# Moving P@V, both units' scores and the sine to even slots in a fused top-k attention and cosine-gated feed-forward kernel

## The chip, the cores and the metric

The kernel runs on one core of a Trainium2 chip. The metric is the device time of one execution in microseconds (us); the time of the kernel before is the median of three runs. Beside the times there is a profile of one execution, with the start and duration of each instruction on each engine: PE is the matrix engine (PEld its loading of weights), DVE the vector engine, ACT the scalar engine, POOL the general-purpose engine, SP the engine that issues most of the transfers.

## The reference

Top-k attention on 8 batches, 8 heads, 576 tokens, head dimension 64, followed by a feed-forward block on the 4608 x 512 result:

```python
scores = scale * np.matmul(q, k.transpose(0, 1, 3, 2))
kth = np.partition(scores, -top_k, axis=-1)[..., -top_k:-top_k + 1]   # top_k = 32
scores = np.where(scores >= kth, scores, -1000000000.0)
scores = scores - np.max(scores, axis=-1, keepdims=True)
attn = np.exp(scores)
attn = attn / (np.sum(attn, axis=-1, keepdims=True) + 1e-09)
x = np.matmul(attn, v)              # -> (4608, 512) after the heads are joined
h = x @ w_in                        # 512 x 2048
g = h * np.cos(h)
out = g @ w_out                     # 2048 x 512
```

## The kernel before

The work is cut into 144 **units**: 128 tokens by one pair of heads. Four units (`hp` 0 to 3) with the same tokens make a **block**, of which there are 36; one in nine lies across two batches, and its units have two `parts`. One unit starts per **slot**. In the long middle stretch a unit u has its top-k search on DVE in slot u, its mask and exponentials on ACT in slot u + 1, its normalisation and the way through DRAM that transposes it in the slots after, and then P@V for two units at once. When the four units of a block are through, its feed-forward is fed to PE in small items: eight "up" items (`ff1`) and eight "down" items (`ff2`) for each block. Each engine works through its instructions in the order in which the program issues them, so the order in `slot` is the order on each engine.

The way of a unit from the normalisation to P@V (`halves` has one buffer, `pT` three):

```python
    def normalise(u):
        s, rden = u["s"], u.pop("rden")
        for j in range(2):
            nc.gpsimd.tensor_scalar(
                out=s[:, j], in0=s[:, j], scalar1=rden[:, j : j + 1], scalar2=1.0,
                op0=ALU.mult, op1=ALU.mult,
            )

    def split(u):


        s = u.pop("s").rearrange("p j k -> p (j k)").bitcast(U16)
        halves = work.tile([P, 2, 2 * S], U16, tag="halves", name="halves", bufs=1)
        nc.gpsimd.tensor_copy(out=halves, in_=s.rearrange("p (k h) -> p h k", h=2))
        u["halves"] = halves

    def write_halves(u):
        rows = u["rows"] = dram.tile([P, 2, 2 * S], U16, tag="rows", name="rows")
        nc.sync.dma_start(out=rows, in_=u.pop("halves"))

    def transposes(u):
        rows = u.pop("rows").rearrange("q h k -> (q h) k")
        pT = u["pT"] = work.tile([P, 2 * NT + 1, P], F32, tag="pT", name="pT", bufs=3)
        words = pT.rearrange("p c q -> p (c q)").bitcast(U16)
        nc.sync.dma_start_transpose(
            out=words.rearrange("p (c q) -> p c q", c=2 * NT + 1), in_=rows
        )
    # ...
    def values(us):      # P@V of two units into one PSUM region: 20 matmuls for each unit
    # ...
```

The feed-forward between the two matmuls. `take_first` copies a bank from PSUM (`L478`); four up items fill one `g` tile; its sine argument is reduced on POOL, the sine taken on ACT, and the product taken on POOL:

```python
    def take_first(blk, g, mm, half):
        nc.scalar.mul(out=g[:, half * 512 : half * 512 + 512], in_=mm, mul=INV_2PI)
        if half == 1:
            fresh.append([blk, g])

    def take_banks():
        while full:
            take, *what = full.popleft()
            take(*what)

    def reduce_first():

        if not fresh:
            return
        blk, g = fresh[0]
        x = ffw.tile([P, 1024], F32, tag="x", name="x", bufs=XB)
        fresh[0].append(x)
        if ff["end"]:

            nc.vector.tensor_scalar(
                out=x, in0=g, scalar1=0.25, scalar2=MAGIC, op0=ALU.add, op1=ALU.add
            )
            nc.vector.scalar_tensor_tensor(
                out=x, in0=x, scalar=MAGIC, in1=g, op0=ALU.subtract, op1=ALU.subtract
            )
            return
        gp = nc.gpsimd
        gp.tensor_scalar(out=x, in0=g, scalar1=1.0, scalar2=0.25, op0=ALU.mult, op1=ALU.add)
        gp.tensor_scalar(out=x, in0=x, scalar1=1.0, scalar2=MAGIC, op0=ALU.mult, op1=ALU.add)
        gp.tensor_scalar(out=x, in0=x, scalar1=-MAGIC, scalar2=1.0, op0=ALU.add, op1=ALU.mult)

    def reduce_second():
        if not fresh or len(fresh[0]) < 3:
            return
        blk, g, x = fresh.popleft()
        if not ff["end"]:
            nc.gpsimd.tensor_tensor(out=x, in0=g, in1=x, op=ALU.subtract)
        waiting.append((blk, g, x, ff["now"], -TWO_PI_BELOW if ff["end"] else TWO_PI_BELOW))

    def sines(least):

        n = sum(c[3] < ff["now"] for c in waiting)
        if n == 0 or (n < least and waiting[0][3] + 2 > ff["now"]):
            return
        for _ in range(n):
            blk, g, x, _, scale = waiting.popleft()
            nc.scalar.activation(out=x, in_=x, func=AF.Sin, bias=halfpi, scale=scale)
            sined.append((blk, g, x))

    def gate(n):
        for _ in range(min(n, len(sined))):
            blk, g, x = sined.popleft()
            eng = nc.vector if ff["end"] else nc.gpsimd
            eng.tensor_tensor(out=g, in0=g, in1=x, op=ALU.mult)
            blk["gated"].append(ff["tick"])
```

How many items a slot feeds, and which (`tick` counts the calls of `feed`):

```python
    def can_first():
        if not first:
            return False
        blk, i = first[0]
        if blk["left"] or ff["tick"] < blk["tick"] + 2 or wq["ready"] < (((i + 1) * (256 // blk["w"]) - 1) // FC + 1) * NC:
            return False
        return i % 4 > 0 or ff["live"] + staged() < CHUNKS
    def can_second():
        if not second:
            return False
        blk, i, f = second[0]
        lag = 3 if 5 * NP < ff["now"] < NU - NP else 2
        gated = sum(ff["tick"] >= t + lag for t in blk["gated"])
        return gated * 1024 // blk["w"] >= f + 2 and wq["ready"] >= NC * NF // FC + f + 2
    def feed(n):
        ff["tick"] += 1
        while n > 0 and ff["credit"] >= 1:
            for kind in (ff["kind"], 1 - ff["kind"]):
                if (can_first, can_second)[kind]():
                    break
            else:
                return
            if kind == 0:
                ff1(*first.popleft())
            else:
                ff2(*second.popleft())
            if kind != ff["kind"] or ff["half"]:
                ff["kind"], ff["half"] = 1 - kind, 0
            else:
                ff["half"] = 1
            n, ff["credit"] = n - 1, ff["credit"] - 1
    # per slot: ff["credit"] = min(ff["credit"] + 5.0 - 0.9 * len(scored.get(i, [])), 5.3)
```

A slot of the middle stretch, and what it is called with:

```python
    EARLY, LAST = 2 * NP, NU - NP
    scored, last, last_values = {}, {}, {}
    for i, u in enumerate(units):
        two = i % 2 and EARLY + 2 < i < LAST + 2 and len(u["parts"]) == 1
        scored.setdefault(i - 2 if two else i - 1, []).append(u)
        for part in u["parts"]:
            last[part[0], u["hp"]] = i - 2 if two else i - 1
            last_values[part[0], u["hp"]] = i
    # ...
    def slot(i, u, w, x, y, z):
        if x:
            reciprocal(x)
        if u:
            topk_first(u, w)
            decode_second(2)
        if u:
            topk_round(u, 1)
            topk_round(u, 2)
            topk_round(u, 3)
        if z:
            values(z)
        made = scored.get(i, [])
        if z:
            take_banks()
        else:
            feed(1)
        for m in made:
            scores(m)
        late = len(made) > 0
        if w:
            bounds(w)
            mask(w)
        take_banks()
        if w and late:
            exponentials(w)
        if z:
            take_values(z)
        take_scores(units[i + 1])
        if w and not late:
            exponentials(w)
        for load, b, hp in at_slot.get(i, []):
            load(b, hp)
        load_weights(2)
        if y:
            transposes(y)
        gate(1)
        if x:
            normalise(x)
            split(x)
            write_halves(x)
        feed(2)
        take_banks()
        decode_third()
        decode_first(2)
        reduce_first()
        reduce_second()
        feed(1 if len(made) == 2 else 3)
        if i % 2:
            sines(1)
        elif i < EARLY + 8 or i > LAST - 2:
            sines(2)
    # ... the loop over the slots:
        u, w = (units[i - n] if 0 <= i - n < NU else None for n in range(2))
        x, y = (units[i - n] if EARLY <= i - n < LAST else None for n in range(2, 4))
        z = units[i - 5 : i - 3] if i % 2 and EARLY <= i - 5 < LAST else None
```

The first nine slots (`early_slot`) and the last four (`last_slot`) transpose on PE and use the same parts in another order.

Of the kernel before, what the change touches and what calls it, by code (L numbers as in the profile page):

```python
# [31 lines left out]
def kernel(  # L32
# [16 lines left out]
    NP = H // 2  # L49
# [35 lines left out]
    for i in range(DF // CW):  # L85
        w = consts.tile([P, NC, CW], F32, tag=f"w_in{i}", name=f"w_in{i}")
# [4 lines left out]
    for f in range(NF):  # L91
        w = consts.tile([P, DM], F32, tag=f"w_out{f}", name=f"w_out{f}")
# [3 lines left out]
    ff = {"live": 0, "tick": 0, "now": 0, "credit": 0.0, "end": False, "kind": 0, "half": 0, "open": 0}  # L96
# [58 lines left out]
    units = []  # L155
    for t0 in range(0, B * S, P):
        parts = []
# [183 lines left out]
    def reciprocal(u):  # L341
        u["rden"] = small.tile([P, 2], F32, tag="rden", name="rden")
        nc.vector.reciprocal(u["rden"], u.pop("den"))  # L343
# [19 lines left out]
# [11 lines that stand above are left out]
# [113 lines left out]
# [26 lines that stand above are left out]
            nc.gpsimd.tensor_tensor(out=x, in0=g, in1=x, op=ALU.subtract)  # L513
        waiting.append((blk, g, x, ff["now"], -TWO_PI_BELOW if ff["end"] else TWO_PI_BELOW))

    def sines(least):

        n = sum(c[3] < ff["now"] for c in waiting)
        if n == 0 or (n < least and waiting[0][3] + 2 > ff["now"]):
            return  # L520
        for _ in range(n):
# [10 lines that stand above are left out]
# [36 lines left out]
    def can_second():  # L568
        if not second:
            return False  # L570
        blk, i, f = second[0]

        lag = 3 if 5 * NP < ff["now"] < NU - NP else 2
        gated = sum(ff["tick"] >= t + lag for t in blk["gated"])
        return gated * 1024 // blk["w"] >= f + 2 and wq["ready"] >= NC * NF // FC + f + 2

# [18 lines that stand above are left out]
# [8 lines left out]
    EARLY, LAST = 2 * NP, NU - NP  # L603
    scored, last, last_values = {}, {}, {}
    for i, u in enumerate(units):
        two = i % 2 and EARLY + 2 < i < LAST + 2 and len(u["parts"]) == 1
        scored.setdefault(i - 2 if two else i - 1, []).append(u)
        for part in u["parts"]:
            last[part[0], u["hp"]] = i - 2 if two else i - 1
            last_values[part[0], u["hp"]] = i  # L610
    at_slot = {}
    order = [(b, hp) for b in range(B) for hp in range(NP)]
    for n in range(NP, len(order)):
        i = last[order[n - 5]] if n >= 5 else 0
        at_slot.setdefault(max(i, NP + 2), []).append((load_qk, *order[n]))
        i = last_values[order[n - 6]] if n >= 6 else 0
        at_slot.setdefault(max(i + 5 - i % 2, NP + 2), []).append((load_v, *order[n]))

    for hp in range(NP):
        at_slot.setdefault(hp, []).append((load_v, 0, hp))  # L620
# [44 lines left out]
        feed(2)  # L665
        sines(2)

    def slot(i, u, w, x, y, z):
        if x:
            reciprocal(x)  # L670
        if u:
# [29 lines that stand above are left out]
        for load, b, hp in at_slot.get(i, []):  # L701
            load(b, hp)
        load_weights(2)
        if y:
            transposes(y)
        gate(1)
        if x:
            normalise(x)
            split(x)
            write_halves(x)  # L710
        feed(2)
        take_banks()
        decode_third()
        decode_first(2)
        reduce_first()
        reduce_second()
        feed(1 if len(made) == 2 else 3)
        if i % 2:
            sines(1)
        elif i < EARLY + 8 or i > LAST - 2:  # L720
            sines(2)

    def last_slot(i, u, w, x, y, z):
        if x:
            reciprocal(x)
        if u:
# [9 lines that stand above are left out]
        if i + 1 < NU:  # L736
            scores(units[i + 1])
        if z:
            take_values(z)
        if i + 1 < NU:  # L740
            take_scores(units[i + 1])
        if y:
            transposes(y)
        if x:
            normalise(x)
            split(x)
            write_halves(x)
        reciprocal(w)
        normalise(w)
        if u:  # L750
            topk_round(u, 2)
            topk_round(u, 3)
        gate(2)
        feed(2)
        transposes_now(w)
# [4 lines that stand above are left out]
        values([w])  # L760
        take_values([w])
        feed(2)
# [10 lines left out]
    for i in range(NU + 1):  # L773
        ff["end"] = i >= NU
        ff["credit"] = min(ff["credit"] + 5.0 - 0.9 * len(scored.get(i, [])), 5.3)
        ff["now"] += 1
        wq["ready"] = wq["done"]
        u, w = (units[i - n] if 0 <= i - n < NU else None for n in range(2))
        x, y = (units[i - n] if EARLY <= i - n < LAST else None for n in range(2, 4))
        z = units[i - 5 : i - 3] if i % 2 and EARLY <= i - 5 < LAST else None  # L780
        if i <= EARLY:
            early_slot(i, u, w)
        elif i <= LAST:
            slot(i, u, w, x, y, z)
        else:
            last_slot(i, u, w, x, y, z)
    while first or second or full:
        ff["now"] += 1
        ff["credit"] = 2.0
# [44 lines left out]
```

## Time and profile before

| | us |
|---|---|
| median of three runs | 1522.23 (1521.3 to 1523.08) |
| span of the profiled execution | 1521.9 |
| busy: PE / DVE / ACT / POOL | 1417.3 / 1416.0 / 1149.2 / 1102.9 |
| one top-8 search of DVE (`MAX8`, 288 wide), mean | 0.447 |
| one fold of DVE (`L244`), mean | 0.752 |
| mean granted PE clock, share of full speed | 0.966 |

How to read the lines shown below. A line of the timeline gives the start, the time from the first start to the last end of a group, the engine, the line of the kernel, the operation with output and input, and how many instructions the group has; brackets name the idle time ahead of it and what ended that. In the table by stretch each engine has its busy time and, in brackets, its instructions; the last three numbers are the granted PE clock, the share of time in which the transfer engines were busy, and GB/s. The list of transfers ends with the median time from issue to landing. The list of waits has the total, the count and the longest. A down item is four instructions of `L543`, an up item sixteen of `L465`, since each matrix product shows as two instructions.

### The profile page before, as it was taken

To read this page: it belongs to the slowest core of one execution; us is meant where nothing else is said; L and a number is where in the kernel's file an instruction comes from. 1 tells how busy PE (TensorE), PEld (TensorE's weight loads), DVE (VectorE), ACT (ScalarE), POOL (GpSimd) and SP (SyncE) were. 2 spreads that over 40 slices of the span, in tenths; PEclk is the share of its full clock that TensorE was granted. 3 is DMA by queue.
4 is the path that set the end of the run, shared out by engine and by line. 5 is a ranking of instruction groups with operands and counts; after the bars stand their busy time and mean duration, and the time that the engine had idled before them with its cause. 6 is when DMAs were issued, how large, how long until landed. Compare 5 with 4: busy or idle time off the path is not lost.

```text
span 1521.9 us, 30207 instructions
## 1 busy us (share of the span) xinstructions
PE 1417.3 (93%) x10360; PEld 1020.5 (67%) x10360; DVE 1416.0 (93%) x4690; ACT 1149.2 (76%) x2322; POOL 1102.9 (72%) x837
## 2 busy tenths in 40 slices
PE   4567798999999999999999999999999999999899
PEld 3365365676777767777777767777777767776774
DVE  7989999999999999999999999999999999999521
ACT  7888766777777778877777777777777777777631
POOL 4777966778777778777777777777777777776500
PEclk6587999999999999999999999999999999999899
DMA  8422364645655555646655456555664455545000
GB/s 265 139 83 83 99 178 135 186 117 175 161 169 132 132 148 164 179 132 156 165 170 132 132 151 168 171 133 152 167 171 132 132 151 158 151 132 132 17 15 14
DMA packets 371753, 212.20 MB, mean 139 GB/s; under 512 B 321296, under 2 KB 337936, under 8 KB 371600
## 3 DMA queue, kind: packets, MB, share of 16 engines
q1 hardware_dynamic: 366192, 200.63, 48.7%
q10 hardware_dynamic: 5408, 9.65, 1.9%
q8 instruction: 81, 1.33, 0.4%
q14 instruction: 72, 0.59, 0.1%
HBM read 45.09 MB, written 87.29 MB: 87 GB/s over the span
## 4 chain that ended last, share of the span: by engine, by line
DVE 74%; PE 12%; ACT 6%; issue 3%; POOL 2%; DMA 2%; SPq 1%; DVEq 0%; ACTq 0%; POOLq 0%
DVE top L304 33%; DVE rest L307 27%; DVE rest L244 11%; PE o L543 5%; PE mm L465 4%; PE rim L408 2%; ACT s L334 1%; DVE top L292 1%; ACT s L326 1%; DVE top L297 1%; DVE w_out L138 1%; PE sc L220 1%; DMA pT<-rows 1%; DVE rden L343 1%; ACT st L127 1%
## 5 line engine op out<-in xcount | busy, mean ns | idle before, releaser
L304 DVE MAX8 top<-rest 128x8 f32<-128x288 f32 (+1 forms) x1656 | 681.2, 460 | 0.0
L465 PEld LDWEIGHTS mm<-xT,w_in 128*128 128x128 f32 x4608 | 536.3, 193 | 83.4 <-ACT g L478 39.8
L465 PE MATMUL mm<-xT,w_in 128*128 128x128 f32 x4608 | 546.9, 277 | 7.4 <-ACT g L478 3.4
L543 PE MATMUL o<-w_out,g 128*128 128x512 f32 x1152 | 532.1, 605 | 11.3 <-POOL g L530 5.6
L307 DVE MATCH_REPLACE8 rest<-top,rest 128x288 f32<-128x288 f32 (+1 forms) x1104 | 494.6, 455 | 0.0
L348 POOL TENSOR_SCALAR s<-s,rden 128x576 f32<-128x576 f32 x288 | 212.7, 750 | 259.1 <-DVE rden L343 259.1
L543 PEld LDWEIGHTS o<-w_out,g 128*128 128x128 f32 x1152 | 209.3, 192 | 232.4 <-issue 210.4
L360 POOL COPY halves<-s 128x2304 uint16<-128x2304 uint16 x132 | 277.7, 2103 | 27.4 <-DMA rows<-halves 19.9
L334 ACT ACTIVATE s<-s,nd 128x576 f32<-128x576 f32 x288 | 219.7, 764 | 0.8
L244 DVE TENSOR_TENSOR rest<-sc,s 128x576 f32<-128x576 f32 x264 | 198.5, 752 | 10.2 <-ACT s L231 2.7
L326 ACT ACTIVATE s<-s,nb 128x576 f32<-128x576 f32 x288 | 205.3, 760 | 0.0
L314 ACT ACTIVATE nb<-top 128x4 f32<-128x4 f32 x144 | 29.6, 206 | 230.2 <-DVE top L297 229.6
L408 PE MATMUL rim<-pT,v 128*64 128x128 f32 (+1 forms) x2560 | 163.1, 272 | 21.5 <-ACT pT L389 13.7
L530 POOL TENSOR_TENSOR g<-g,x 128x1024 f32<-128x1024 f32 x67 | 158.3, 2363 | 22.3 <-ACT nb L314 11.4
L220 PE MATMUL sc<-k,q 64*128 64x448 f32 (+1 forms) x640 | 150.1, 583 | 17.0 <-DMA k<-in_k_dram 9.3
L513 POOL TENSOR_TENSOR x<-g,x 128x1024 f32<-128x1024 f32 x68 | 161.0, 2367 | 5.7
L408 PEld LDWEIGHTS rim<-pT,v 128*64 128x64 f32 x2560 | 134.4, 141 | 38.3 <-ACT pT L389 16.3
L230 ACT COPY s<-sc 128x896 f32<-128x896 f32 x144 | 129.0, 896 | 3.3 <-PE sc L220 3.3
L478 ACT ACTIVATE g<-mm 128x512 f32<-128x512 f32 x144 | 83.7, 583 | 54.3 <-PE mm L465 43.9
L220 PEld LDWEIGHTS rim<-k,q 64*128 64x128 f32 (+1 forms) x640 | 57.3, 180 | 57.8 <-issue 52.7
L523 ACT ACTIVATE x<-x,halfpi 128x1024 f32<-128x1024 f32 x72 | 82.5, 1149 | 6.9 <-DVE x L499 6.1
L523 ACT ACT_TABLE_LOAD x66 | 84.7, 1283 | 1.6 <-ACT ob L553 0.4
(55 smaller groups left out, 1232.0 us busy)
## 6 DMA issues: line engine op xcount, KB each, us to landing
rows<-halves SPq DMA_DIRECT2D x132, 576.0 KB, 3.2
out_dram<-ob ACTq DMA_DIRECT2D x36, 256.0 KB, 2.9
q<-in_q_dram SPq DMA_DIRECT2D x31, 288.0 KB, 3.3
st<-in_moe_w_in_dram SPq DMA_DIRECT2D x16, 512.0 KB, 5.8
v<-in_v_dram SPq DMA_DIRECT2D x32, 256.0 KB, 3.9
st<-in_moe_w_out_dram SPq DMA_DIRECT2D x16, 512.0 KB, 3.6
k<-in_k_dram SPq DMA_DIRECT2D x31, 144.0 KB, 3.4
k<-in_k_dram SPq DMA_DIRECT2D x32, 128.0 KB, 3.8
```

The source lines that it names most:

```text
L220: nc.tensor.matmul(to[r0 : r0 + rows, j, 0 : k1 - k0], st["q"][d, q0 : q0 + rows], st["k"][d, k0:k1], start=True, stop=True,)
L244: nc.vector.tensor_tensor(out=u["rest"][:, :, i * HS : (i + 1) * HS], in0=sc[:, :, 0:HS], in1=s[:, :, HS:S], op=op,)
L304: nc.vector.max(to[:, j], src[:, j])
L307: nc.vector.match_replace(rest[:, j], to[:, j], src[:, j], NEG)
L326: nc.scalar.activation(out=s[:, j], in_=s[:, j], func=AF.Prelu, bias=nb[:, j, 1:2], scale=SCALE, alpha=FAR)
L334: nc.scalar.activation(out=s[:, j], in_=s[:, j], func=AF.Exp, bias=nd[:, j : j + 1], scale=1.0, accum_out=den[:, j : j + 1],)
L348: nc.gpsimd.tensor_scalar(out=s[:, j], in0=s[:, j], scalar1=rden[:, j : j + 1], scalar2=1.0, op0=ALU.mult, op1=ALU.mult,)
L360: nc.gpsimd.tensor_copy(out=halves, in_=s.rearrange("p (k h) -> p h k", h=2))
L408: nc.tensor.matmul(o[d, to], lhsT, rhs, start=c == 0, stop=c == NT)
L465: nc.tensor.matmul(mm[:, at : at + w], w_in[f // FC][:, c, (f % FC) * P : (f % FC + 1) * P], blk["xT"][:, c], start=c == 0, stop=c == NC - 1,)
L523: nc.scalar.activation(out=x, in_=x, func=AF.Sin, bias=halfpi, scale=scale)
L543: nc.tensor.matmul(o, g[:, at : at + P], w_out[f], start=f == 0, stop=f == NF - 1)
```

## The change

P@V of a pair of units and the scores of two units move from odd to even slots, and P@V is taken one slot earlier after its units' normalisation. The transpose is issued in the same slot as the write that it reads. In even slots the argument of the sine is computed ahead of the normalisation, and the sine follows at the end of the same slot. The wait of down items for the product (`lag`) is lengthened from slot 12 on instead of slot 20. It is meant to shorten the way from a unit's scores to the feed-forward.

```diff
--- before.py
+++ after.py
@@ -513,9 +513,9 @@
             nc.gpsimd.tensor_tensor(out=x, in0=g, in1=x, op=ALU.subtract)
         waiting.append((blk, g, x, ff["now"], -TWO_PI_BELOW if ff["end"] else TWO_PI_BELOW))
 
-    def sines(least):
-
-        n = sum(c[3] < ff["now"] for c in waiting)
+    def sines(least, since=1):
+
+        n = sum(c[3] <= ff["now"] - since for c in waiting)
         if n == 0 or (n < least and waiting[0][3] + 2 > ff["now"]):
             return
         for _ in range(n):
@@ -570,7 +570,7 @@
             return False
         blk, i, f = second[0]
 
-        lag = 3 if 5 * NP < ff["now"] < NU - NP else 2
+        lag = 3 if 3 * NP < ff["now"] < NU - NP else 2
         gated = sum(ff["tick"] >= t + lag for t in blk["gated"])
         return gated * 1024 // blk["w"] >= f + 2 and wq["ready"] >= NC * NF // FC + f + 2
 
@@ -603,7 +603,7 @@
     EARLY, LAST = 2 * NP, NU - NP
     scored, last, last_values = {}, {}, {}
     for i, u in enumerate(units):
-        two = i % 2 and EARLY + 2 < i < LAST + 2 and len(u["parts"]) == 1
+        two = i % 2 == 0 and EARLY + 2 < i < LAST + 2 and (len(u["parts"]) == 1 or u["hp"] == 0)
         scored.setdefault(i - 2 if two else i - 1, []).append(u)
         for part in u["parts"]:
             last[part[0], u["hp"]] = i - 2 if two else i - 1
@@ -614,7 +614,7 @@
         i = last[order[n - 5]] if n >= 5 else 0
         at_slot.setdefault(max(i, NP + 2), []).append((load_qk, *order[n]))
         i = last_values[order[n - 6]] if n >= 6 else 0
-        at_slot.setdefault(max(i + 5 - i % 2, NP + 2), []).append((load_v, *order[n]))
+        at_slot.setdefault(max(i + 4 - i % 2, NP + 2), []).append((load_v, *order[n]))
 
     for hp in range(NP):
         at_slot.setdefault(hp, []).append((load_v, 0, hp))
@@ -665,7 +665,7 @@
         feed(2)
         sines(2)
 
-    def slot(i, u, w, x, y, z):
+    def slot(i, u, w, x, z):
         if x:
             reciprocal(x)
         if u:
@@ -701,26 +701,29 @@
         for load, b, hp in at_slot.get(i, []):
             load(b, hp)
         load_weights(2)
-        if y:
-            transposes(y)
-        gate(1)
+        if i % 2 == 0:
+            reduce_first()
+            reduce_second()
         if x:
             normalise(x)
             split(x)
             write_halves(x)
+            transposes(x)
+        gate(1)
         feed(2)
         take_banks()
         decode_third()
         decode_first(2)
-        reduce_first()
-        reduce_second()
+        if i < EARLY + 8:
+            reduce_first()
+            reduce_second()
         feed(1 if len(made) == 2 else 3)
-        if i % 2:
+        if i % 2 == 0:
+            sines(1, 0)
+        elif i < EARLY + 8:
             sines(1)
-        elif i < EARLY + 8 or i > LAST - 2:
-            sines(2)
-
-    def last_slot(i, u, w, x, y, z):
+
+    def last_slot(i, u, w, x, z):
         if x:
             reciprocal(x)
         if u:
@@ -739,12 +742,11 @@
             take_values(z)
         if i + 1 < NU:
             take_scores(units[i + 1])
-        if y:
-            transposes(y)
         if x:
             normalise(x)
             split(x)
             write_halves(x)
+            transposes(x)
         reciprocal(w)
         normalise(w)
         if u:
@@ -776,14 +778,14 @@
         ff["now"] += 1
         wq["ready"] = wq["done"]
         u, w = (units[i - n] if 0 <= i - n < NU else None for n in range(2))
-        x, y = (units[i - n] if EARLY <= i - n < LAST else None for n in range(2, 4))
-        z = units[i - 5 : i - 3] if i % 2 and EARLY <= i - 5 < LAST else None
+        x = units[i - 2] if EARLY <= i - 2 < LAST else None
+        z = units[i - 4 : i - 2] if i % 2 == 0 and EARLY <= i - 4 < LAST else None
         if i <= EARLY:
             early_slot(i, u, w)
         elif i <= LAST:
-            slot(i, u, w, x, y, z)
+            slot(i, u, w, x, z)
         else:
-            last_slot(i, u, w, x, y, z)
+            last_slot(i, u, w, x, z)
     while first or second or full:
         ff["now"] += 1
         ff["credit"] = 2.0
```

## The prediction

> **What bounds the kernel now.** I read the busy times first, then the busy time by stretch, then one pair of slots in the timeline, engine by engine.
>
> ```profile
> PE 1417.3 (93%) x10360; PEld 1020.5 (67%) x10360; DVE 1416.0 (93%) x4690; ACT 1149.2 (76%) x2322; POOL 1102.9 (72%) x837
> ```
>
> Two engines are level, so an average does not tell which one is the bound. By stretch:
>
> ```profile
> 200.00:400.00 200.00, 184.72 (x1480) 135.06 (x1477) 194.99 (x683) 146.55 (x309) 145.40 (x109) 0.98 0.58 160
> ...
> 600.00:800.00 200.00, 199.87 (x1541) 146.39 (x1540) 198.86 (x694) 159.99 (x323) 157.73 (x117) 1.00 0.60 160
> ...
> 1440.00:1480.00 40.00, 40.00 (x261) 29.86 (x260) 9.69 (x11) 14.66 (x29) 6.40 (x6) 1.00 0.02 7
> ```
>
> The columns are PE, PEld, DVE, ACT, POOL. In the middle both PE and DVE are full; in the last 80 us PE works alone on feed-forward left over. Is PE's fullness real? One pair of slots:
>
> ```profile
> 810.16 1.04 PE L408 MATMUL rim<-pT,v 128*64 128x128 f32 x16
> ...
> 813.50 3.70 PE L543 MATMUL o<-w_out,g 128*128 128x512 f32 x8
> 817.04 3.73 PE L465 MATMUL mm<-xT,w_in 128*128 128x128 f32 x32
> 820.61 3.60 PE L543 MATMUL o<-w_out,g 128*128 128x512 f32 x8
> 824.27 3.84 PE L465 MATMUL mm<-xT,w_in 128*128 128x128 f32 x32
> 828.04 1.10 PE L408 MATMUL rim<-pT,v 128*64 128x128 f32 x16
> ```
>
> The groups start back to back, and the same 32 and 8 instructions take as long in the tail, where nothing holds them. So it is real. The pair repeats after 828.04 - 809.02 = 19.02 us (809.02 is the start of the first unit's P@V); the vector engine's slots start at 800.77, 810.29 and 819.79, also 19.02 a pair. PE has eight feed items in a pair (813.50 to 828.04, so 1.82 us each), P@V of two units and scores of two: 18.98 us. **PE can be delayed once, but it can never catch up.** The last `L465` group of a pair ends just ahead of the next P@V; it completes a `g` tile. Next the Pool engine:
>
> ```profile
> 810.53 1.47 POOL L348 TENSOR_SCALAR s<-s,rden 128x576 f32<-128x576 f32 x2 [3.64 <-DVE rden L343]
> 812.06 2.10 POOL L360 COPY halves<-s 128x2304 uint16<-128x2304 uint16 x1
> 814.13 1.04 POOL L504 TENSOR_SCALAR x<-g 128x1024 f32<-128x1024 f32 x1
> ...
> 817.53 2.37 POOL L513 TENSOR_TENSOR x<-g,x 128x1024 f32<-128x1024 f32 x1
> 819.93 2.36 POOL L530 TENSOR_TENSOR g<-g,x 128x1024 f32<-128x1024 f32 x1
> 822.28 1.47 POOL L348 TENSOR_SCALAR s<-s,rden 128x576 f32<-128x576 f32 x2
> ```
>
> Normalise and split take 3.6 us from start to end. Sine's argument (four instructions) takes 819.93 - 814.13 = 5.80. Now it stands **behind** the normalisation, so nothing of attention waits for it. The way out of Pool is write, then transpose:
>
> ```profile
> 806.92 0.34 SPq L365 DMA_DIRECT2D rows<-halves  x1
> 809.77 3.20 SPq L371 DMA_TRANSPOSE pT<-rows  x1
> ```
>
> ```profile
> pT<-rows SPq DMA_TRANSPOSE x132, 4.8
> POOL halves L360 <- DMA rows<-halves: 19.9, 14, 4.6
> ```
>
> The transpose goes out 2.85 us after the write, as soon as that has landed, and lands 4.8 us later in the median (4.3 to 6.9). The second line: `halves` has one buffer, and a split close behind another already waits for the write.
>
> [...] a normalisation emitted behind a product `L530` starts behind it (822.28 above). So what is moved ahead of the normalisation holds it. [...]
>
> **The change, part by part.**
>
> *Transpose issued with its write.* Same instructions. Before, it stood a slot later in the program but already left at 2.85 us behind its write. Alone it is worth nothing; it only no longer has the next slot's loads in front of it.
>
> *P@V and both scores in even slots, P@V one slot earlier.* Same instructions. In slot i PE now takes units i-4 and i-3, where it took i-5 and i-4. The gain: a block's feed-forward starts a slot earlier. Stepping through `feed`'s credits and ticks by hand from slot 9 on, I get 476 items open at slot 35 before and 469 after (slot 17 is blocked in the new order, but later losses vanish). Both then do exactly eight a pair (three with P@V, five without, with the credit capped at 5.3), so the lead of seven stays to the end: 7 x 1.82 = **12.7 us less tail**. The `lag` of 3 from slot 12 on is met exactly by gates of the slot before last and stops nothing later. The cost: unit i-3 is normalised in slot i-1 and needed at once. In an undisturbed odd slot, normalise starts 0.24 us after the slot, the write goes at 3.9, the transpose at 6.75, landing at 11.4, and a slot is 9.5: ready 1.9 us **into** the next slot, while PE came to the second unit 0.13 us ahead of it (810.16 against 810.29). So PE falls back at least 2 us against DVE; that much the buffers between scores and the folds take up.
>
> *Sine's argument ahead of the normalisation.* In even slots Pool first takes `g`, whose last matmuls end just ahead of that slot's P@V, and only then normalises. This closes a **loop**: P@V of the odd unit -> the eight items -> `g` -> argument -> even unit's split -> odd unit's split -> write -> transpose -> P@V two pairs on. Its length:
> - second unit's P@V to the end of the eight items: 828.04 - 810.16 = 17.88
> - copy of `g` from PSUM 0.58 and two handovers of some 0.08: 0.73
> - argument 5.80; even normalise and split 3.63: 9.43
> - the odd split waits until the even write has landed (`halves`): 2.90; the split: 2.10
> - the queue is then still in the even transpose (2.90 + 2.6 against 5.00): 0.50
> - the odd write landed, behind a transpose (241.95 to 245.39 in the queue's timeline): 3.44
> - transpose landed: 4.6
>
> Sum 41.6 us for two pairs, where DVE needs 38.04. **The loop is 3.5 us too long**, so a pair takes 20.8 us, 1.75 more. If the two transfers don't hold each other up, it is 40.5, or 20.25 a pair: 1.2 more. I take the middle, 1.5. From slot 20 (full rate) to 140 there are 60 pairs: 90 us, less some 2 us that PE may fall back before DVE waits.
>
> *Sine beside the scores.* Sine follows its argument in the same even slot. It was beside the two scores before as well, with two table loads a pair (1.28 us each); this stays, only in the other slot. Pool's argument would be ready 6.5 us after `g`, about when ACT gets there. No cost of its own.
>
> **Sum.** 1522.2 + 90 - 2 - 12.7 = 1597.5; I say 1598.
>
> **The rivals.**
> 1. *The loop does not bind.* The change then brings its 12.7 us: about 1510. For it: each earlier stage shortens the pipeline, and the lag fits the new order exactly. Against it: it asks the loop to be 3.5 us shorter than durations measured in this very trace. One way would be that the feed ended a pair with `o` and not with `mm` items: `g` would be ready 3.6 us earlier. By hand I find the order 22 1 | 1 22 11 (1 for up, 2 for down), with `mm` last, as in the trace above.
> 2. *It binds a little*, say 0.5 us a pair, if the `halves` wait and the queue's wait vanish because DVE's own delay spreads the two splits: 30 - 12.7, about 1540.
> 3. *ACT becomes the bound*: `g` is copied first in an even slot, ahead of the thresholds, so a late PE also delays mask, exponentials and the copy of the next scores. From `g` to the end of that copy I count some 6.2 us, so DVE starts odd slots no earlier. This is how the loop reaches DVE and no second loss.
>
> **Range and chances.** The loop at 20.25 to 20.9 a pair gives 1580 to 1620; a looser one 1540 to 1580; none 1510. The first is by far the likeliest, so 1538 to 1624 for eight in ten. Faster by over 2% (below 1492) would take far more than the tail can give: 0.03. Within 2% (to 1552.7): rival 1 and the lower part of rival 2, 0.17. Slower: 0.80.
>
> **What would show it.** Right: a pair near 20.5 us in the middle; PE waiting at P@V for `pT<-rows`, about 1.5 us a pair; DVE waiting once a pair at the fold `L244` for the copy of the scores; Pool waiting for `L478` ahead of `L504`, and at the split for `rows<-halves`; the stretch after the last slot some 12 us shorter. Wrong: pairs of 19.02 with P@V waiting once and not again (rival 1); DVE waiting elsewhere, for `den` or `nb`, with `pT` long landed; or a tail that is not shorter, which would make my count of items wrong.

## The result, and the profile after

The kernel after the change takes 1708.8 us (median of four runs, 1702.94 to 1711.04) against 1522.47 us for the kernel before, measured beside it: a ratio of **1.122 (95% interval 1.119 to 1.1248)**, slower by 186 us. The prediction was 1598 us, with 1538 to 1624 as its range. The direction and the mechanism came as predicted; the size did not.

The busy times after:

```profile
PE 1475.0 (87%) x10360; PEld 1063.7 (63%) x10360; DVE 1420.9 (84%) x4689; ACT 1161.6 (68%) x2326; POOL 1106.3 (65%) x838
```

The vector engine (DVE) does the same work in nearly the same time (1416.0 before), and it is no longer full. The matrix engine (PE) has the same 10360 instructions but is busy 58 us longer, so some of them have become slower. Two lines make up 55 of the 58 us: P@V (`L408`, 163.1 us before and 187.7 after) and the scores (`L220`, 150.1 and 180.7). By stretch (columns as before: PE, PEld, DVE, ACT, POOL, then the granted PE clock):

```profile
200.00:400.00 200.00, 170.75 (x1275) 124.12 (x1276) 169.12 (x591) 132.03 (x268) 125.55 (x93) 0.91 0.49 132
600.00:800.00 200.00, 180.09 (x1334) 129.51 (x1330) 167.03 (x582) 134.59 (x269) 130.94 (x98) 0.93 0.49 133
```

In the middle no engine is full any more. A stretch in which every engine has gaps is bound by a chain that runs through several of them. The waits after, as engine, line, releaser, total us, count, longest:

```profile
POOL x L504 <- ACT nb L314: 280.7, 62, 8.5
...
POOL halves L360 <- DMA rows<-halves: 145.8, 64, 7.0
...
PE rim L408 <- DMA pT<-rows: 144.8, 51, 5.5
DVE rest L244 <- ACT s L231: 140.6, 37, 7.6
```

They stood at 4.5 (put down to `L478` itself), 19.9, 3.4 and 2.7 us before. The first three belong to one ring: Pool's argument waits for `g` (the scalar engine's `L314` follows `L478` by 0.1 us and is named for it), the split waits for the write, and P@V for the transpose. The fourth hangs on it: DVE waits for scores that PE made too late. One passage of that ring, from the chain of waits of the kernel after (start, us, what):

```profile
1122.40 2.40 PE rim L408 x20
...
1139.08 3.59 PE mm L465 x32
...
1142.68 0.60 ACT g L478
...
1143.38 1.05 POOL x L504
...
1146.78 2.37 POOL x L513
1149.14 1.47 POOL s L348 x2
...
1150.66 2.11 POOL halves L360
...
1152.80 3.17 DMA rows<-halves
...
1156.08 2.11 POOL halves L360
...
1158.21 3.39 DMA rows<-halves
...
1161.68 4.44 DMA pT<-rows
...
1166.16 2.40 PE rim L408 x20
```

P@V to P@V is 1166.16 - 1122.40 = 43.76 us for four slots, where DVE had needed 38.04. DVE appears nowhere in it.

**Where the 179 us between the two profiled executions (1521.9 and 1701.2) lie.** DVE starts each slot with a reciprocal, so its n-th reciprocal is a clock of progress (from the 8th on, reciprocal n opens slot n + 2):

| reciprocal, counted from 0 | before, us | after, us | behind by |
|---|---|---|---|
| 12 | 188.11 | 198.55 | 10.4 |
| 18 | 245.17 | 267.14 | 22.0 |
| 60 | 648.57 | 727.31 | 78.7 |
| 138 | 1390.79 | 1587.62 | 196.8 |
| 143 (last of DVE) | 1448.29 | 1640.47 | 192.2 |
| end of the program | 1521.9 | 1701.2 | 179.3 |

So 22 us are lost in the first full slots (the fill), 174.9 us in the 120 slots of the middle, which is 44.02 us for four slots instead of 38.19. The last five slots bring 4.6 us back, and the stretch after the last reciprocal is shorter: 60.7 against 73.6 us, 12.9 us gained.

### The profile page after: what moved, and what is told of

It reads as the page before. It is cut to its first block, busy times and chain, and to the rows that moved or that the text cites. A ratio compares the mean times of both kernels' runs of the same rounds, so it can differ in the third digit from the quotient of the medians.

```text
span 1701.2 us, 30203 instructions
## 1 busy us (share of the span) xinstructions
PE 1475.0 (87%) x10360; PEld 1063.7 (63%) x10360; DVE 1420.9 (84%) x4689; ACT 1161.6 (68%) x2326; POOL 1106.3 (65%) x838
## 3 DMA queue, kind: packets, MB, share of 16 engines
q1 hardware_dynamic: 366192, 200.63, 42.5%
## 4 chain that ended last, share of the span: by engine, by line
PE 55%; DMA 20%; POOL 12%; ACT 6%; SPq 4%; issue 2%; DVE 2%; POOLq 0%; ACTq 0%; DVEq 0%
PE o L543 21%; PE mm L465 19%; DMA pT<-rows 11%; DMA rows<-halves 8%; PE rim L408 7%; PE sc L220 7%; POOL halves L360 3%; SPq L371 3%; POOL x L513 3%; POOL s L348 2%; PE rim L220 2%; POOL x L505 1%; POOL x L506 1%; POOL x L504 1%; ACT s L334 1%
## 5 line engine op out<-in xcount | busy, mean ns | idle before, releaser
L360 POOL COPY halves<-s 128x2304 uint16<-128x2304 uint16 x132 | 277.9, 2105 | 150.2 <-DMA rows<-halves 145.8
L408 PE MATMUL rim<-pT,v 128*64 128x128 f32 (+1 forms) x2560 | 187.7, 298 | 167.6 <-DMA pT<-rows 144.8
L244 DVE TENSOR_TENSOR rest<-sc,s 128x576 f32<-128x576 f32 x264 | 198.7, 753 | 143.9 <-ACT s L231 140.6
L408 PEld LDWEIGHTS rim<-pT,v 128*64 128x64 f32 x2560 | 150.9, 155 | 191.5 <-DMA pT<-rows 145.7
L504 POOL TENSOR_SCALAR x<-g 128x1024 f32<-128x1024 f32 x68 | 71.3, 1049 | 286.5 <-ACT nb L314 280.7
L478 ACT ACTIVATE g<-mm 128x512 f32<-128x512 f32 x144 | 85.7, 596 | 202.0 <-PE mm L465 201.8
L414 ACT COPY xT<-rim 128x256 f32<-128x256 f32 (+1 forms) x78 | 27.7, 355 | 234.4 <-PE rim L220 221.5
L220 PE MATMUL sc<-k,q 64*128 64x448 f32 (+1 forms) x640 | 180.7, 703 | 7.5 <-DMA k<-in_k_dram 7.5
L513 POOL TENSOR_TENSOR x<-g,x 128x1024 f32<-128x1024 f32 x68 | 160.6, 2362 | 5.6
L220 PEld LDWEIGHTS rim<-k,q 64*128 64x128 f32 (+1 forms) x640 | 65.9, 212 | 76.3 <-issue 71.3
```

The costliest lines, as they stand in the source:

```text
L220: nc.tensor.matmul(to[r0 : r0 + rows, j, 0 : k1 - k0], st["q"][d, q0 : q0 + rows], st["k"][d, k0:k1], start=True, stop=True,)
L244: nc.vector.tensor_tensor(out=u["rest"][:, :, i * HS : (i + 1) * HS], in0=sc[:, :, 0:HS], in1=s[:, :, HS:S], op=op,)
L408: nc.tensor.matmul(o[d, to], lhsT, rhs, start=c == 0, stop=c == NT)
```

## The experiments

Ratios are to the kernel before. "Four slots" is the mean from reciprocal 18 to reciprocal 138, and the fill loss is how far reciprocal 18 lies behind 245.17.

### Does the argument close the ring?

The kernel after, with the argument of the even slot moved behind the normalisation and everything else kept:

```diff
-        if i % 2 == 0:
-            reduce_first()
-            reduce_second()
         if x:
             normalise(x)
             ...
             transposes(x)
+        if i % 2 == 0:
+            reduce_first()
+            reduce_second()
         gate(1)
```

> The changed kernel with one thing undone: in even slots sine's argument stands behind normalise and split again, still in the same slot. Loop theory: the even unit no longer waits for g, and from g to the next P@V there are only copy 0.7, argument 5.8, odd unit's normalise and split 3.6, write 2.9, transpose 4.6, and 17.9 on PE: 35.5 us of the 38.0 that two pairs have. No loop binds, pairs of 19.0 us, about 1510 us in all (the seven feed items earlier kept, 12.7 us). Rival A, P@V one slot earlier has no room by itself: the loss stays, over 1600. Rival B, ACT: the sine now has to wait some 2 us for its argument in every even slot and holds the next thresholds: about 1570.

Measured: 1567.72 us, ratio 1.0306 (1.0283 to 1.0329). Moving two calls gives back 141 of the 186 us. Of the 30 groups of four slots 21 take 38.0 to 38.5 us again: the ring is gone. The number of rival B (1570) is matched better than mine, but not its reason, since between a few events DVE's slots are regular. The time that is still lost comes mostly near changes of batch (five groups of 43.7 to 48.8 us) and in the fill (20.9 us). SP's own timeline at one change of batch in this kernel:

```profile
928.39 0.60 SPq L188 DMA_DIRECT2D k<-in_k_dram  x1
929.09 0.53 SPq L365 DMA_DIRECT2D rows<-halves  x1
932.35 3.49 SPq L371 DMA_TRANSPOSE pT<-rows  x1
```

The loads of the next `q` and `k` start at 926.83, when PE has done with the old ones (in after SP waits 123.8 us for this, in 21 times: `SPq L185 <- PE rim L220`). They stand ahead of the even write, whose split had ended at 924.34; its transpose, the odd write (935.94) and the odd transpose (939.98) follow late, and the second unit's P@V waits 2.19 us at 944.42 and then takes 1.56 us, where 1.04 to 1.09 is usual.

The other half of the pair: the kernel before, with the argument ahead of the normalisation in odd slots from slot 17 on.

```diff
+        if i % 2 and i >= EARLY + 8:
+            reduce_first()
+            reduce_second()
         gate(1)
         if x:
             normalise(x)
```

> The kernel before with one part of the change: in its odd slots from 17 on sine's argument stands ahead of normalise and split. Loop theory: the unit so delayed has its P@V only two slots later, the way from g to it is 17.6 us plus 17.9 on PE, 35.5 of 38.0, so nothing binds: 1522, within 5. Rival: an argument ahead of the normalisation costs by itself, because every normalisation behind it is 5.8 us later: some 2 us or more a pair, 1640.

Measured: 1523.79 us, ratio 1.0008 (0.9995 to 1.0021). Alone the argument ahead costs nothing. It needs P@V one slot earlier to become a ring. P@V one slot earlier without the argument ahead is the run above: no ring, but 45 us slower.

The last small part alone: the kernel before with the transpose issued right behind its write.

```diff
             write_halves(x)
+            transposes(x)
```

> The kernel before with one part of the change alone: the transpose issued right behind its write. As it already leaves 2.85 us behind the write, nothing changes but its place against the loads: 1522, within 4. If the place in the queue matters, by what loads hold up, a few us faster; if the transpose now holds the loads back, a few slower.

Measured: 1520.49 us, ratio 0.9995 (0.9986 to 1.0003): no effect, as it had already left when the write landed (2.85 us behind it, at 809.77 in before).

### Do the loads take part in the ring?

Three kernels without the loads of `q`, `k` and `v` for seven of the eight batches (the tiles of the first batch are used again, so they compute another result): after, after with the argument behind, and before.

```diff
+        if b:
+            st["q"], st["k"] = pairs[0, hp]["q"], pairs[0, hp]["k"]
+            return
```

(and the same for `v`).

> The changed kernel without the loads of q, k and v for seven of the eight batches (every batch uses the first one's; the loads are the work left out, all else is there). It measures what the loads add to the loop. If the loop alone makes the loss, the pairs still take 21 to 22 us: 1660 to 1690. If the loads are most of it, as where only the argument is put back: under 1600.

> The same left out from the run with the argument behind the split. If the loads ahead of the writes are all that run loses in the middle (43 us) and half of what it loses early (20 us), 1505 to 1518 are left, below the kernel before, because the tail is 13 us shorter. If P@V one slot earlier has a wait of its own: 1540 or more.

> The same left out from the kernel before, as the measure for the two others. Its loads lie beside other work and P@V is a slot later, so little should change: 1517 to 1523.

| | us | ratio | four slots, us | fill loss, us |
|---|---|---|---|---|
| after, no loads | 1709.08 | 1.1227 (1.117 to 1.1283) | 44.12 | 20.6 |
| after, argument behind, no loads | 1514.07 | 0.9956 (0.994 to 0.9972) | 38.09 | 14.6 |
| before, no loads | 1520.24 | 0.9993 (0.9984 to 1.0001) | 38.14 | -0.8 |

I had expected the first to fall to 1660 to 1690. It did not move: **the ring alone costs the whole middle**. The second is the important one. With neither ring nor loads the new order is 6 us faster than the old one without loads, and its P@V waits, in the list of waits of that kernel (whose lines are numbered six higher), have shrunk from 144.8 us to

```profile
PE rim L414 <- DMA pT<-rows: 15.6, 16, 5.3
```

So P@V one slot earlier is bearable in the middle, and what the argument behind left at 1567.72 us was mostly loads: 53.7 us between the two.

### Three ways out of the loads

Loads behind write and transpose, first in after, then with the argument behind as well:

```diff
-        for load, b, hp in at_slot.get(i, []):
-            load(b, hp)
-        load_weights(2)
         ...
             transposes(x)
+        for load, b, hp in at_slot.get(i, []):
+            load(b, hp)
+        load_weights(2)
```

> The changed kernel (argument still ahead) with the loads of q, k and v issued behind the slot's write and transpose instead of ahead of them. Second theory, the queue: in slots with loads the even write waits behind loads that themselves wait for that slot's scores on PE, some 3 us where it happens, in about half the pairs. Then some 60 x 0.5 x 3 / 2 = 45 us go, about 1660. If the loads cost nothing beside the loop: 1705.

> Both undone: argument behind the split, and loads behind write and transpose. In the run with the argument behind alone, plain pairs took 19.0 us, and 6 to 10 us were lost where q and k of a new batch are loaded. If the loads ahead of the write are the rest of the loss, these go too and the seven feed items remain: 1510 to 1525, equal to the kernel before or a little faster. If PE's waits there have another cause (the early slots, or k landing late): 1550 or more.

Measured: in after 1764.73 us, ratio 1.1615 (1.1585 to 1.1645), so **worse**, against my expectation; with the argument behind 1532.37 us, ratio 1.0063 (1.0042 to 1.0083). Why worse, in SP's timeline of the first:

```profile
1145.42 2.30 SPq L371 DMA_TRANSPOSE pT<-rows  x1
...
1151.43 0.58 SPq L365 DMA_DIRECT2D rows<-halves  x1
```

Between them go six loads of `v`. Pool had ended the odd split at 1147.59, so the odd write starts 3.8 us late. In this passage the loads lengthen the ring itself; four slots take 46.1 us in the mean, where after took 44.0. Without the ring the same order takes 38.7 us, against 39.6 with the loads ahead.

On top of the better of the two: no early argument before slot 16, and the loads of `v` in odd slots; then the loads of `q` and `k` issued by ACT instead of SP.

```diff
-        if i % 2 == 0:
+        if i % 2 == 0 and i >= EARLY + 8:
             reduce_first()
...
-        at_slot.setdefault(max(i + 4 - i % 2, NP + 2), []).append((load_v, *order[n]))
+        at_slot.setdefault(max(i + 5 - i % 2, NP + 2), []).append((load_v, *order[n]))
... second kernel only:
-            nc.sync.dma_start(out=q, in_=qs)
+            nc.scalar.dma_start(out=q, in_=qs)
```

> The run with argument behind and loads later, with two more edits: before slot 16 the argument is not taken early in the slot, and the loads of v move to odd slots. That run lost 10 us by slot 12 (in its slots 10 and 11 DVE's weight decoding, L137 and L138, took 22 us where it took 15 before, beside POOL's argument) and 15 us in the middle, 2 to 3 us at each change of batch. If the decoding is slow because POOL works beside it, some 3 to 6 us come back; with the v loads out of the even slots some more: 1520 to 1527. If neither matters: 1532.

> The same, with the loads of q and k for all batches but the first issued by ACT, so that no load stands between a write and a transpose of attention in SP's queue in even slots. If the rest of the loss in the middle is the queue, the pairs stay at 19.0 throughout and the seven items of feed-forward remain as gain: 1510 to 1518. If the 2 us of issuing on ACT, or its wait for the buffer, hold the thresholds, it is 1525 or more.

Measured: 1534.16 us, ratio 1.0082 (1.0053 to 1.0112), and 1564.63 us, ratio 1.0281 (1.0256 to 1.0306). The first missed its expectation: nothing gained, the fill loss still 12 us. In the second ACT is held up where it issues the loads: its waits ahead of the sine's table load that are put down to issuing come to 31.9 us, the longest 11.6, and the first kernel has none of these. The exponentials behind wait with it: DVE's wait for `den` is 61.0 us in 26 times against 38.6 in 25 for the first. What the issuing itself waits for is not shown.

### How much of the ring is the slow PE, and how much the single `halves`?

The kernel after answers part of this itself, as its groups of four slots differ in the granted PE clock (third number from the end). Two of the 30, each from one reciprocal to the fourth behind it:

```profile
837.41:878.98 41.57, 37.83 (x275) 27.41 (x274) 37.90 (x132) 30.48 (x61) 29.89 (x22) 1.00 0.54 150
...
1095.93:1140.71 44.78, 40.18 (x275) 29.17 (x274) 37.87 (x132) 30.57 (x61) 29.95 (x22) 0.92 0.45 118
```

Five groups had the full clock and took 41.05 to 41.93 us, 41.43 in the mean. Six with a clock of 0.96 took 42.8 to 44.4 us, and nineteen with 0.92 or 0.93 took 43.5 to 47.0. In after without loads, where no load stands in the way, the order is the same: 42.5 to 43.4 us at 0.96 (five groups) and 43.8 to 45.2 at 0.92 (the other 25). As an estimate from the two means, the slow PE costs (44.02 - 41.43) x 30 = 78 of the 174.9 us of the middle, and the ring at full clock the rest.

A kernel that should keep the clock up: after, with twelve small transposes that nobody reads between the P@V of the first and of the second unit, so that PE idles less:

```diff
         for i, u in enumerate(us):
+            if i == 1:
+                for _ in range(12):
+                    nc.tensor.transpose(room[1][:, 0:P], ident, ident)
             pT = u.pop("pT")
```

> The changed kernel with twelve small transposes into an unused part of PSUM between the P@V of the first and of the second unit, some 1.3 us of PE work a pair in the place where PE waits for pT. If a wait of over 3 us makes PE run slower after it (in the changed kernel P@V and scores after such a wait take 6.05 us where 3.46 us are usual), the waits left are shorter and the loop falls from 43.8 toward 41.6 us for two pairs: about 1640. If the slow instructions have another cause, such as pT being read while it lands, nothing is gained: 1705 or more.

Measured: 1686.43 us, ratio 1.1087 (1.1059 to 1.1114); mean granted clock 0.952, where after has 0.918. Idle work makes the kernel 22 us faster. In PE's timeline (lines three higher):

```profile
1163.90 1.16 PE L411 MATMUL rim<-pT,v 128*64 128x128 f32 x16 [3.07 <-DMA pT<-rows]
...
1165.42 1.87 PE L220 MATMUL sc<-k,q 64*128 64x448 f32 x4
```

P@V is quick again here (1.16 instead of 1.97 us), the scores behind it are still slow (1.87 us, where 1.02 is usual). They do not read `pT`, so a `pT` that is read while it lands does not explain them. In 18 of the 30 groups the clock is full throughout, and these take 41.5 to 42.8 us; the other twelve take 44.3 to 48.9. Where the clock held, the expectation came true; it held too seldom for 1640 us.

After with two `halves` buffers (and two argument buffers fewer, to make room):

```diff
-        ... tag="halves", name="halves", bufs=1)
+        ... tag="halves", name="halves", bufs=2)
-    CHUNKS, XB = 8, 4
+    CHUNKS, XB = 8, 2
```

> The changed kernel with two buffers for halves (and two instead of four for the sine's argument, to make room). In the chain the wait for the even write is 3.3 us, of which 1.5 lie beside the odd normalise. Loop theory: the odd write then waits in the queue behind the even transpose, which itself waits for the even write and holds the queue to 5.3 to 5.5 us behind the even split, just where the odd write goes today: no gain, 1700 to 1710. Rival: the buffer is the limit and its 1.8 us are gained in every two pairs: about 1655.

Measured: 1725.69 us (two runs), ratio 1.135 (1.1308 to 1.1392). No gain, as expected, but 16 us over the upper end of my range: the split no longer waits, but the queue does. In one passage the even write goes at 1166.20, the even transpose takes the queue from 1169.43 to 1171.83, and the odd write, whose split had ended at 1169.79, goes at 1171.88. From even to odd write that is 5.7 us, and 5.4 in after. I don't know what makes it 1% worse; the smaller number of argument buffers was not tried alone.

### The fill

ACT's timeline of the kernel after, at the end of slot 12:

```profile
189.98 1.15 ACT L523 ACTIVATE x<-x,halfpi 128x1024 f32<-128x1024 f32 x1 [5.84 <-POOL x L513]
```

Pool is still decoding weights until 184.2 and has the argument ready at 189.95. The sine "beside the scores" stands in ACT's order ahead of the next slot's mask and exponentials, so these wait with it, and DVE waits 7.39 us for `den` at 198.55. After with argument and sine as in the kernel before up to slot 16, and then the same with the argument behind throughout and the loads of `q`, `k` and `v` (not of weights) behind the transpose:

```diff
-        if i % 2 == 0:
+        if i % 2 == 0 and i >= EARLY + 8:
             reduce_first()
...
-        if i % 2 == 0:
-            sines(1, 0)
-        elif i < EARLY + 8:
-            sines(1)
+        if i < EARLY + 8:
+            sines(1 if i % 2 else 2)
+        elif i % 2 == 0:
+            sines(1, 0)
```

> After, with the first seven of the full slots (before slot 16) as in the kernel before in two things: the argument behind the normalisation, and the sine one slot later. Theory (sine in the same slot stands in ACT's queue ahead of the next slot's mask and exponentials, while Pool is still decoding weights): ACT's wait of 5.8 us for the argument at 184 us and DVE's wait of 7.4 us for den in the slot at 198.55 go, and the 18th reciprocal starts 8 to 14 us sooner than 267.1, near 256; the middle stays at 44 us for four slots; about 1698 in all. Rival (the fill loss comes from P@V being one slot earlier, or from the decoding on DVE that waits for Pool): the 18th reciprocal stays at 263 to 269, about 1708.

> After, with the argument behind the normalisation in all slots, the loads of q, k and v (not of the weights) behind write and transpose, and before slot 16 argument and sine as in the kernel before. Theory of the sine: against the kernel with only the first two of these (1532.4) the 8.1 us that ACT waits for the argument near 182 us and the 6.7 us that it waits for weights near 150 us go, and the loss by the 18th reciprocal falls from 13 to 3 or less: 1518 to 1524. Rival: the loss by the 18th reciprocal stays at 11 to 13 us: 1530 to 1534.

Measured: 1724.88 us, ratio 1.1319 (1.1283 to 1.1354), and 1531.15 us, ratio 1.0055 (1.0035 to 1.0074). Each of the two expectations is half right. The two waits do go: reciprocal 12 starts at 191.31 instead of 198.55, so 7.2 of the 10.4 us up to there were the sine and its argument. Beside that wait, after lost time where DVE decodes weights: `L137` and `L138` took 5.19 and 3.22 us behind reciprocals 8 and 9, where they took 2.66 and 2.45 before. But by reciprocal 18 the first kernel is 19.5 us behind again, the second 9.9. What takes over fits the rival, a P@V that is now needed one slot earlier. PE's timeline of the second:

```profile
199.80 1.97 PE L408 MATMUL rim<-pT,v 128*64 128x128 f32 x16 [7.64 <-DMA pT<-rows]
```

The unit in question was normalised at 187.70, late behind Pool's own `L513`, and its write went only at 191.37, while P@V one slot earlier now asks for it at once; DVE then waits 5.5 us for scores. In the first of the two the middle also takes 44.7 us for four slots instead of 44.0; this I have not explained.

No kernel with all of the work is measurably faster than the one before; the best one with the new P@V is at 1.0055.

## Why the prediction was wrong

- **The tail, 12.7 us less: right.** 12.9 us were measured, and counting the items by hand had been worth it.
- **The transpose issued with its write is worth nothing: right** (0.9995 alone).
- **PE falls back by P@V one slot earlier, and "that much the buffers between scores and the folds take up": right in the middle** (38.09 us for four slots without ring and loads), **wrong in the fill**, where the way through Pool is longer (7.64 us of wait in the last kernel above).
- **The loop: right as a mechanism, its members in the order named.** Only the wait for the queue was not there: the even transpose held it for 2.04 us, not 2.6. Member by member, in one passage:

| step of the sum | predicted, us | measured, us |
|---|---|---|
| second P@V to the end of the eight items | 17.88 | 20.26 |
| copy and handovers | 0.73 | 0.72 |
| argument, even normalise and split | 9.43 | 9.39 |
| wait for the even write (1152.77 to 1156.08) | 2.90 | 3.31 |
| odd split | 2.10 | 2.11 |
| the queue still in the even transpose | 0.50 | 0 |
| odd write landed | 3.44 | 3.41 |
| transpose landed | 4.6 | 4.56 |
| sum | 41.6 | 43.76 |

- **The step that failed: the first term of the sum, 17.88 us on PE from the second unit's P@V to the end of the eight items.** It was measured in a kernel whose PE never pauses. In the ring PE waits for `pT` and is slow when it starts again: P@V and scores took 6.05 us (1122.40 to 1128.44) where 3.32 is usual (half of the pair's P@V, 2.33 us at 1097.86, and 2.15 of scores), and the term came to 20.26 us. All other terms together came out 0.2 us shorter than predicted. Where the clock stayed full the sum was right: 41.43 us in the mean of five groups, against 41.6. "I take the middle, 1.5" allowed for members that might hide and cost little: 3.0 us for four slots where 41.43 - 38.19 = 3.24 was measured, 7 us in 30 groups. The slow PE costs some 78. With the 90 us predicted that makes 175, the loss of the middle. PE's timeline in after shows it, the same sixteen matmuls in the first and in the second unit:

```profile
1116.48 1.09 PE L408 MATMUL rim<-pT,v 128*64 128x128 f32 x16
...
1122.40 1.97 PE L408 MATMUL rim<-pT,v 128*64 128x128 f32 x16 [4.60 <-DMA pT<-rows]
```

  and the table by stretch, ahead of the wait and behind it, has the granted clock (third number from the end) at half:

```profile
1110.00:1117.80 7.80, 7.80 (x59) 5.76 (x58) 7.76 (x27) 6.12 (x15) 4.97 (x3) 1.00 0.66 198
...
1122.40:1128.40 6.00, 6.00 (x37) 4.14 (x37) 2.12 (x9) 0.00 (x0) 5.63 (x6) 0.55 0.15 61
```

  So the wait of 4.60 us is followed by a clock of 0.55, while waits of 1.20 and 2.22 us (at 800.55 and 821.68) leave the group at 1.09 us. Length alone does not decide it: in after the clock was 0.64 in the 4 us behind the wait of 2.09 us that ended at 925.30, and 1.00 behind the one of 2.94 us that ended at 904.30. With the argument behind, the group took 1.56 us behind the wait of 2.19 us at 944.42. I had predicted PE's wait and then used PE's durations from a trace without it.
- **"No cost of its own" for the sine: right in the middle, wrong in the fill, and no term at all for the fill.** ACT waits for Pool's argument once in the whole run, 5.84 us, and that is in the fill. The fill cost 22 us, of which 7.2 come from the sine and its argument ahead of reciprocal 12 and some 3 from slower decoding on DVE; most of the others look like P@V one slot earlier while Pool still decodes, which no run isolates.
- **The rivals.** Rival 1, about 1510 us, is what the change brings without ring and loads: 1514.07. Rival 2 fails, as the wait at `halves` did not vanish (145.8 us). Rival 3 looks rightly judged: DVE waits for scores (140.6 us) and for `den` (79.5 us), and ACT is in the passage above only with the copy of `g`; no run tests it alone. Of the signs named, the waits of PE, Pool and DVE came; PE's were 144.8 us, some 2.4 a pair and not 1.5, and in the passage above they come once in two pairs.

The loads at batch changes, a fourth limit that I had not named, cost nothing inside the ring (1709.08 without them) and 54 us as soon as the ring is gone. That is how one hidden limit stands behind another.

## What to carry to other kernels

When a change makes two stages wait for each other in turn, write the ring down, add its members and compare the sum with what the period should be; here the full sum was within 0.2 us of the ring at full clock. Then ask what the new wait does to the durations themselves, above all of an engine that had never paused. Test the parts of such a change one by one: here the argument ahead cost nothing alone, P@V one slot earlier 45 us, and the two together 186. Undoing one of them gave back 141 us; idle work for PE gave back 22, and a second buffer nothing.

## What the runs showed of the hardware

- In after, between 260 and 1440 us, PE had 21 waits of 2.89 us or more (up to 5.5). Behind 20 of them the mean granted clock was 0.50 to 0.62 for 4 us, behind the one of 2.94 us it was 1.00. After the wait of 4.60 us the mean was 0.55 for 6 us, and a matmul group took 1.97 us instead of 1.09. Of the waits under 2.0 us none was followed by a lower clock, and of the five in between (2.09 to 2.57 us) two were: 0.64 behind 2.09 us and 0.63 behind 2.49 us.
- A vector-engine decode of 512 words in after took 0.41 us where Pool was idle (at 106.90), but 2.60 us beside a Pool operation with two tensors, and ended 0.28 us behind it:

```profile
149.04 2.60 DVE L137 TENSOR_SCALAR w_out<-w_out 128x512 f32<-128x512 f32 x1
```

```profile
148.93 2.43 POOL L513 TENSOR_TENSOR x<-g,x 128x1024 f32<-128x1024 f32 x1
```

  The ends are at 151.64 and 151.36 us. A decode at 118.35 (`L138`) took 2.45 us beside the same Pool operation and ended 0.28 us behind it too (120.80 and 120.52). What held the decodes is not shown. In the slot of the fill the 2.2 us more show as DVE's busy time and in no list of waits.
- A transpose held the issuing queue for 2.2 to 2.9 us (after, 400 to 700 us, 28 transposes). With two `halves` buffers it was this that held up the second unit's write, which went at 1171.88, 2.1 us behind the end of its split.
